# Maxima of the norms ahead of the additions on VectorE, and an output load that is divided and issued sooner, in a four-layer attention and spectral kernel

## The chip, the cores and the metric

The kernel runs on one core of a Trainium2 chip. The metric is the device time of one execution in microseconds (us), as the median of several runs; lower is better. A core has TensorE (matmuls, PE in the profile), VectorE (DVE), ScalarE (ACT) and GpSimd (POOL), which run side by side and wait for each other through semaphores. SyncE (SP) issues most of the transfers between HBM and the on-chip memory (SBUF). Matmul results land in eight banks of PSUM.

## What is computed

x has 2048 rows of 1024 numbers. Four residual layers follow each other: attention, spectral, attention, spectral.

```python
def _A_ref(x, wqkv, wo):
    qkv = (x @ wqkv).reshape(B, S, 3, H, Dh).transpose(2, 0, 3, 1, 4)   # H = 32 heads of 32
    q, k, v = qkv[0], qkv[1], qkv[2]
    scores = jnp.einsum("bhqd,bhkd->bhqk", q, k) * (Dh ** -0.5)
    p = _softmax(scores, axis=-1)
    o = jnp.einsum("bhqk,bhkd->bhqd", p, v)
    return o.transpose(0, 2, 1, 3).reshape(B, S, D) @ wo

def _B_ref(x, w_r, w_i):
    X = jnp.fft.rfft2(x, axes=(-2, -1)) * (w_r + 1j * w_i)
    return jnp.fft.irfft2(X, s=(S, D), axes=(-2, -1))

x = x + _A_ref(_layernorm(x), A_wqkv, A_wo)
x = x + _B_ref(_layernorm(x), B_w_r, B_w_i)      # and both once more
```

The change lies in the attention layers.

## The kernel before

**Groups, chunks, units.** The 32 heads are treated in 8 head groups of 4 (g = 0 to 7). A group's 2048 queries are cut into 4 chunks c of 512, its 2048 keys into 16 tiles kt of 128. One pair (c, kt) is a *unit*, numbered u = 16 c + kt, 64 in a group. `S` computes the scores of a unit for four heads on TensorE (line 720) and their exponentials on ScalarE, in two halves of 128x1024 (line 724). These halves p lie in a pool of 8 buffers, that is four units deep. In every even unit `PV` multiplies the p of the two units before with V (line 730).

**Additions.** The softmax's denominators need the sum of p over the keys. `add` builds it on VectorE, two instructions of 128x1024 a unit (line 741 for the first two tiles of a chunk together, line 743 after that), each into the same accumulator `acc`. The code writes the addition of a unit two units after it: in even units that of the first of the last pair, in odd units that of the second. In the first unit of a chunk both open additions are written.

**Projections beside the attention.** Q, K and V of the next groups are computed in the same loop. `filler` yields these matmuls in pieces and `slots` hands out one piece (a slot) in every odd unit: beside an even group K and Q of the next one and K of the one after, beside an odd group Q of the next and V of the next two. One projection of 512 columns is a *sum* (24 matmuls, line 411 for Q and K, 468 for V), usually spread over three slots. All sums share one PSUM buffer x. For Q and K it is emptied by `split`: the high half on ScalarE (line 215), the low half on VectorE (line 216). For V ScalarE alone empties it (line 472). The next sum's first matmul waits for that.

**Norms.** The exponentials use a bound instead of a running maximum. When the four sums of a group's K or Q are done, `norms` sums the squares over each head with four small matmuls (line 443) into a PSUM buffer of the scores' pool, which has three, and takes their maximum on VectorE (line 445); for Q GpSimd then makes the bias. `ripe` says when: one slot later in even groups, two slots later in odd ones and in group 6. So in groups 1 to 5 they fall in units 25 and 45 (even groups) and 3 and 27 (odd groups), in group 6 in units 43 and 47. `slots` calls them before its piece of matmuls, and that is after the unit's addition is written.

**Order.** Within the main loop the order of TensorE and ScalarE is that of the code. VectorE, GpSimd and SyncE are ordered by the planner, which goes through the program in a model of time and takes for each of them the first instruction in the program that is ready. `tc.issue_after(i)` adds edges to that: what is written inside and runs on the engine of i is put behind i in that engine's order. It is no wait.

**Outputs.** A chunk's output is normalized and stored to HBM (`od`) as a task: `tasks` holds pairs of a least kt and a function, in the order in which they come, and `aside` takes the first of them in an odd unit if its kt is reached and no sum ended in that unit. A chunk is stored some 25 units after its end. In group 6 the loop has 22 slots for the sums of group 7 (8 sums), and then begins with the output projection: `wo_parts` reads outputs of the groups 0 to 6 back with `load_o(c)` (line 523, two transfers of seven groups, one for the high and one for the low halves) and multiplies them by Wo (line 531), 7 matmuls a slot. They are laid over the chunk 2 (or 3) of the normalized input, `xhl`, which the projections read until then. `load_wo` converts Wo into the chunks 0 and 1 of it in the same units.

Of the kernel before, what the change touches and what calls it, by code (L numbers as in the profile page):

```python
# [13 lines left out]
AX = mybir.AxisListType  # L14
# [93 lines left out]
NG, NCH, NKT, NST = 8, 4, 16, 6  # L108
# [110 lines left out]
def run(g):  # L219
    for _ in g:  # L220
        pass
# [106 lines left out]
def attention(nc, tc, layer, ap, xin, yd, wts, wo, cst, dram, flags):  # L328
# [5 lines left out]
    od = dram.tile([2, NG, 128, 2048], F16, name=f"od{layer}")  # L334
# [17 lines left out]
    V, K, Q, bias, nrm, mx = {}, {}, {}, {}, {}, {}  # L352
# [15 lines left out]
    def turn_x(xn):  # L368
        p = psS.tile([128, 2, 512], F32, name="s").rearrange("p h (d n) -> p (h d) n", n=128)
        for d in range(8):  # L370
            nc.tensor.transpose(p[:, d], xn[:, 128 * d:128 * d + 128], cst["ident"])
        return p
# [57 lines left out]
    def ripe():  # L430
        if not left_norms:
            return False
        old = left_norms[0] not in fresh or (g % 2 == 0 and g < NG - 2)
        fresh.clear()
        return old

    def norms():
        kind, g = ph = left_norms.pop(0)
        if g not in mx:
            mx[g] = sm.tile([128, 2], F32, name="mqk")  # L440
        ps = psS.tile([128, 2, 512], F32, name="s")
        for c in range(4):
            nc.tensor.matmul(ps[32 * c:32 * c + 32, 0], cst["bones"], nrm[ph][:, c], start=True, stop=True)
        i = 0 if kind == "k" else 1
        nc.vector.reduce_max(mx[g][:, i:i + 1], ps[:, 0], axis=AX.X)  # L445
        if kind == "q":
            mkbias(g)

    def mkbias(g):
        r = sm.tile([128, 2], F32, name="mall")  # L450
        nc.gpsimd.partition_all_reduce(r, mx[g], 128, bass.bass_isa.ReduceOp.max)
        b = sm.tile([128, 1], F32, name="bpr")
        nc.gpsimd.tensor_tensor(b, r[:, 0:1], r[:, 1:2], op=ALU.mult)
        nc.gpsimd.tensor_tensor(b, b, cst["half"], op=ALU.pow)
        bias[g] = sm.tile([128, 1], F32, name="bias")
        nc.gpsimd.tensor_scalar(bias[g], b, -SCALE / (SQ * SQ), None, op0=ALU.mult)
# [23 lines left out]
    def sums(ph):  # L480
        return 8 if ph[0] == "v" else 4
# [35 lines left out]

    osb, olast = {}, {}

    def load_o(c):  # L520
        osb[c] = xhl[:, 2 + c % 2]
        for i in range(2):
            nc.sync.dma_start(osb[c][:, i, 0:7], od[i, 0:7, :, c * 512:(c + 1) * 512].rearrange("g p n -> p g n"))

    def wo_mm(p, c, t, n, ds, start=True, stop=True, w=512):

# [18 lines left out]
    def wo_part(c, t, dst, nd):  # L545

        x = xres(c, t)
        st = sm.tile([128, 2, 6], F32, name="st")
        for n in range(2):
            p = bank()  # L550
            m = wo_mm(p, c, t, n, range(nd))
            for _ in range(3 * nd - 1):
                next(m)
                yield
            run(m)
            sl = slice(n * 512, n * 512 + 512)
            nc.vector.scalar_tensor_tensor(dst[:, sl], p, 1.0 / (SO * SW), x[:, sl], op0=ALU.mult, op1=ALU.add)
            if nd == 8:
                nc.vector.bn_stats(st[:, n], dst[:, sl])
                if n:  # L560
                    r0 = c * 512 + t * 128
                    nc.sync.dma_start(yd[r0:r0 + 128, :], dst)
                    nc.vector.bn_aggr(mvs[:, 8 * c + 2 * t:8 * c + 2 * t + 2], st)
            yield
# [14 lines left out]
    wo_dst = [ap.x[:, 10 + t if t in SPILL else t] for t in range(8)] + [None] * 2 + [ap.x[:, t] for t in (10, 11)]  # L579

    def wo_parts():
        load_o(0)
        for t in (2, 3, 0, 1, 4, 5, 6, 7, 8, 9, 10, 11):
            if t == 8:
                two = wvp.tile([128, 2, 1024], F32, name="wv")
                wo_dst[8], wo_dst[9] = two[:, 0], two[:, 1]
            yield from wo_part(t // 4, t % 4, wo_dst[t], 8 if t == 11 else 7)
            if t in (0, 5, 9):
                load_o({0: 1, 5: 2, 9: 3}[t])
# [46 lines left out]
    with tc.manual_schedule(engines={mybir.EngineType.PE, mybir.EngineType.DVE, mybir.EngineType.Activation}):  # L636
# [14 lines left out]
        p = turn_x(xn)  # L651
# [13 lines left out]
        p = turn_x(xn)  # L665
# [4 lines left out]
        p = turn_x(xn)  # L670
# [5 lines left out]
        p = turn_x(xn)  # L676
# [60 lines left out]
    def add(g, c, kt):  # L737
        for hf in range(2):
            p, a = P[g, c, kt, hf], acc[c % 2][:, hf]
            if kt == 1:  # L740
                last_add = nc.vector.scalar_tensor_tensor(a, P[g, c, 0, hf], 1e-34, p, op0=ALU.add, op1=ALU.add)  # L741
            elif kt:
                last_add = nc.vector.tensor_add(a, a, p)  # L743
        return last_add if kt else None
# [43 lines left out]
    def times(g, c, r):  # L788
        nc.vector.scalar_tensor_tensor(r, O[g, c], SO, r, op0=ALU.mult, op1=ALU.mult)
        O[g, c] = r  # L790
# [18 lines left out]
    tasks = []  # L809
# [6 lines left out]
    def slots(f, sums, n, steps):  # L816

        while sums:
            k = max(1, int(n / sums + 0.5))
            m = -(-steps // k)  # L820
            for i in range(0, steps, m):
                while ripe():
                    norms()
                for _ in range(min(m, steps - i)):
                    next(f, None)
                n -= 1
                yield sums - (i + m >= steps)
            sums -= 1

    with tc.manual_schedule(engines={mybir.EngineType.PE, mybir.EngineType.Activation}):  # L830
        for g in range(NG):
            todo = sum(sums(ph) for ph in beside.get(g, []))
            sl = slots(fill, todo, 22 if g == NG - 2 else 32, 24)
            wsl = slots(wof, 4, 10, 21)
            for u in range(NCH * NKT):
                c, kt = divmod(u, NKT)
                S(g, c, kt)
                if g == u == 0:
                    run(last_v)
                if kt % 2 == 0:  # L840
                    for w in pend:
                        PV(*w)
                    late = pend
                    pend = []
                    if kt == 0 and late:
                        for w in late:
                            last_add = add(*w)
                        turned, going = going, []
                        if late[1][0] == NG - 1:
                            done = [late[1][:2]]  # L850
                            fin(*done[0])
                        else:
                            going = [*late[1][:2], partials(*late[1][:2])]
                        if turned:
                            with tc.issue_after(last_add.ins):
                                turned[2] = invert_partials(*turned)
                            tasks += [(5, lambda t=turned: times(*t)), (6, lambda t=turned: out(*t[:2]))]
                        if u and g < NG - 2:
                            tasks.append((1, wts.look))
                        late = []  # L860
                for w in late[:1]:
                    last_add = add(*w)
                late = late[1:]
                if kt == 5 and done:
                    out(*done.pop())
                pend.append((g, c, kt))
                if kt % 2 == 0:
                    continue
                quiet, before = kt > 12, todo
                if todo:  # L870
                    todo = next(sl)
                elif g == NG - 2:
                    if left:
                        run(lwo)
                        left = 0
                    if next(wsl, None) is not None and u == NCH * NKT - 1:
                        run(wsl)
                elif g == NG - 1:
                    if u % 4 == 1:
                        with tc.issue_after(last_add.ins):  # L880
                            wts.look()
                    if moments:
                        f, t = moments.pop(0)
                        f(t)
                    if u // 2 in rests:
                        wo_rest(rests[u // 2])
                    for _ in range(share[u // 2]):
                        next(wof)
                if g == NG - 2 and todo <= 6 and left > (8 if todo > 4 else 0):
                    next(lwo)  # L890
                    left -= 1
                if quiet or todo == before:
                    aside(kt)
        for w in pend:
            PV(*w)
        for w in late + pend:
            add(*w)
        run(wof)
    assert not wts.unseen and not wts.cols and not moments
    with tc.manual_schedule(engines={mybir.EngineType.PE}):  # L900
        ps, xs, folds = [], [xres(3, t) for t in range(4)], fold_rests()
# [577 lines left out]
```

## Time and profile before

| | |
|---|---|
| runs (3) | 3708.29, 3709.03, 3711.51 us; median 3709.03 |
| the profiled execution | 3706.65 us, span of its instructions 3704.9 us |
| granted clock of TensorE | 0.997 |
| matmul busy | 3638.7 us (98%) |
| VectorE, ScalarE, GpSimd busy | 3131.2, 2935.2, 637.5 us |
| exponentials (line 724) | 2048, mean 1112 ns, 2171.0 us |
| additions (line 743) | 1792, mean 1218 ns, 2088.4 us |
| first unit of groups 1, 2, 3 in layer 0 | 279.8, 456.3, 630.9 us |

"Busy" is the time in which an engine executes. A line of the time order gives start, duration, engine, line of the kernel, operation, output<-input and the shape, how many like instructions in a row are merged (x2), and in brackets how long the engine stood idle before it and who released it. Instructions of an engine overlap by a little at their ends, so that the distance of two starts is the better price of one. A waits view has, for each waiting line and its releaser, the total us, the number of times and the longest.

### The profile page before, as it was taken

How to read it: one execution, taken by the hardware profiler on the slowest of the kernel's cores; microseconds unless marked ns; L12 is line 12 of the kernel's file. 1: busy time of each engine (PE TensorE's matmuls, PEld its weight loads, DVE VectorE, ACT ScalarE, POOL GpSimd, SP SyncE). 2: the span in 40 equal slices, each digit the busy share in tenths (PEclk: the TensorE clock that was granted, in tenths of full speed). 3: DMA queues.
4: the chain of work that ended last, by engine and by line, in shares of the span. 5: the costliest groups of instructions: out<-in, count | busy, mean ns of one | idle time of the engine just before them, and what ended most of it. 6: DMA issues, size and time to landing. Idle time of an engine off the chain costs nothing.

```text
span 3704.9 us, 80669 instructions
## 1 busy us (share of the span) xinstructions
PE 3638.7 (98%) x32919; PEld 1628.0 (44%) x32919; DVE 3131.2 (85%) x3800; ACT 2935.2 (79%) x3653; POOL 637.5 (17%) x798
## 2 busy tenths in 40 slices
PE   8999999999999999999999999999999999999998
PEld 5333433343343233378953334333433432333888
DVE  7799899989998988886767998999899889788754
ACT  5788888888888867768747888888888888676686
POOL 1021112111111110014420111111111111100243
PEclk9999999999999999999999999999999999999999
DMA  7122232322222442233151232323222334421423
GB/s 197 21 53 54 50 54 53 62 42 56 47 61 50 97 115 70 77 144 106 58 165 21 53 59 51 57 48 59 45 53 52 61 58 95 103 78 69 177 82 108
DMA packets 203551, 274.33 MB, mean 74 GB/s; under 512 B 75809, under 2 KB 122529, under 8 KB 202145
## 3 DMA queue, kind: packets, MB, share of 16 engines
q1 hardware_dynamic: 164208, 195.06, 16.6%
q0 software_dynamic: 37632, 73.43, 14.0%
q8 instruction: 260, 4.26, 0.5%
q14 instruction: 123, 1.00, 0.1%
q10 hardware_dynamic: 1328, 0.59, 0.1%
HBM read 149.00 MB, written 118.42 MB: 72 GB/s over the span
## 4 chain that ended last, share of the span: by engine, by line


## 5 line engine op out<-in xcount | busy, mean ns | idle before, releaser
L724 ACT ACTIVATE p<-s,bias 128x1024 f32<-128x1024 f32 x2048 | 2171.0, 1112 | 467.0 <-PE s L720 449.4
L743 DVE TENSOR_TENSOR R<-R,p 128x1024 f32<-128x1024 f32 x896 | 1044.2, 1218 | 76.2 <-ACT p L724 74.1
L743 DVE TENSOR_TENSOR acc<-acc,p 128x1024 f32<-128x1024 f32 x896 | 1044.2, 1217 | 57.8 <-ACT p L724 55.9
L730 PE MATMUL o<-p,R 128*32 128x512 f32 x8192 | 985.7, 599 | 0.0
L411 PE MATMUL x<-big,wqk 128*128 128x512 f16 x2880 | 676.4, 380 | 2.9 <-ACT R L472 1.6
L720 PEld LDWEIGHTS <-R 32*128 32x128 f16 x12288 | 229.4, 92 | 744.3 <-issue 628.7
L411 PEld LDWEIGHTS <-wqk 128*128 128x128 f16 x3072 | 275.9, 98 | 418.3 <-issue 127.7
L730 PEld LDWEIGHTS o<-p,R 128*32 128x32 f32 x8192 | 213.8, 109 | 524.6 <-issue 524.6
L720 PE MATMUL s<-Q,R 32*128 32x512 f16 x6144 | 425.4, 378 | 5.5 <-DVE mqk L445 5.5
L720 PE MATMUL s<-R 32*128 32x512 f16 x6144 | 426.8, 378 | 0.2
L468 PE MATMUL x<-wv,big 128*128 128x256 f16 x2784 | 330.7, 275 | 4.1 <-DVE R L216 2.2
L468 PEld LDWEIGHTS <-big 128*128 128x128 f16 x3072 | 290.9, 98 | 96.0 <-issue 55.2
L531 PE MATMUL x<-big 128*128 128x512 f16 x1008 | 232.4, 380 | 5.0 <-DMA big<-od 5.0
L749 POOL DMA_DIRECT2D zd<-R x112 | 93.4, 834 | 699.1 <-DVE z L759 289.4
L531 PEld LDWEIGHTS <-big 128*128 128x128 f16 x1428 | 134.2, 98 | 170.1 <-issue 28.4
L749 POOL DMA_DIRECT2D zd<-acc x112 | 92.4, 825 | 645.6 <-DVE z L759 302.5
L741 DVE SCALAR_TENSOR_TENSOR R<-p 128x1024 f32<-128x1024 f32 x64 | 75.5, 1221 | 97.5 <-ACT p L724 97.5
L752 POOL DMA_DIRECT2D zd<-zd x112 | 89.4, 798 | 367.0 <-DMA zd<-zd 154.3
L1143 DVE TENSOR_TENSOR H<-G,H 128x512 f16<-128x512 f32 (+1 forms) x68 | 46.8, 689 | 99.9 <-ACT H L1142 99.7
L741 DVE SCALAR_TENSOR_TENSOR acc<-p 128x1024 f32<-128x1024 f32 x64 | 75.8, 1221 | 45.6 <-ACT p L724 45.6
L1085 ACT COPY U<-ps 64x256 f32<-64x256 f32 (+1 forms) x272 | 97.2, 357 | 8.1 <-PE ps L1092 3.0
L1085 ACT COPY B<-ps 64x256 f32<-64x256 f32 (+1 forms) x272 | 97.1, 357 | 5.6 <-PE ps L1092 2.1
(459 smaller groups left out, 3291.5 us busy)
## 6 DMA issues: line engine op xcount, KB each, us to landing
zd<-R POOLq DMA_DIRECT2D x112, 256.0 KB, 4.1
zd<-acc POOLq DMA_DIRECT2D x112, 256.0 KB, 4.2
wst<-in_wp SPq DMA_DIRECT2D x96, 256.0 KB, 3.4
R<-y SPq DMA_DIRECT2D x32, 512.0 KB, 5.8
w<-in_w SPq DMA_DIRECT2D x60, 256.0 KB, 2.7
zt<-zr SPq DMA_DIRECT2D x224, 64.0 KB, 2.7
od<-ohl SPq DMA_DIRECT2D x56, 256.0 KB, 2.4
big<-od SPq DMA_DIRECT2D x16, 896.0 KB, 6.4
```

The source lines that it names most:

```text
L411: nc.tensor.matmul(ps, a, b, start=i == 0, stop=i == 23)
L468: nc.tensor.matmul(ps[:, j], x[c][:, d, o:o + 128], w[:, n, d], start=i == 0, stop=i == 23)
L531: nc.tensor.matmul(p, a, b, start=start and d == ds[0] and i == 0, stop=stop and d == ds[-1] and i == 2)
L720: nc.tensor.matmul(s[h // 2][:, h % 2], K[g][r, a, kt * 128:kt * 128 + 128], Q[g][r, b, c * 512:c * 512 + 512], start=i == 0, stop=i == 2)
L724: nc.scalar.activation(p, s[hf], AF.Exp, bias=bias[g], scale=SCALE / (SQ * SQ))
L730: nc.tensor.matmul(O[g, c][32 * h:32 * h + 32], V[g][:, kt, 32 * h:32 * h + 32], P[g, c, kt, h // 2][:, h % 2], start=kt == 0, stop=kt == ...
L741: last_add = nc.vector.scalar_tensor_tensor(a, P[g, c, 0, hf], 1e-34, p, op0=ALU.add, op1=ALU.add)
L743: last_add = nc.vector.tensor_add(a, a, p)
L749: nc.gpsimd.dma_start(z, a[32 * j:32 * j + 32].rearrange("p a j n -> p (a j n)"), max_dma_last_dim=2048, **({"accum_op": ALU.add} if j els ...
L752: nc.gpsimd.dma_start(z[0:n], z[n:2 * n], accum_op=ALU.add, max_dma_last_dim=2048)
L1085: nc.scalar.copy(ov[64 * r:64 * r + 64, a0:a0 + m, x], tl[64 * x:64 * x + 64, :m, r])
L1143: nc.vector.tensor_sub(lo, gs, hi)
```

## The change

`norms` returns the instruction of the maximum. It is no longer called by `slots` but by the main loop in each odd unit, ahead of that unit's addition, and the addition is written behind an edge to the maximum. The matmuls of the norm keep their place on TensorE: after the scores, before the slot's piece.

`load_o` takes a range of groups. The load for chunk 0 is no longer the first step of `wo_parts`: the outputs of the groups 0 to 5 are asked for in group 6 when two of the eight sums are left (the last sum that reads that part of `xhl` has ended then, in unit 33; the first slot of the output projection is unit 45), and those of group 6 as a task with a least kt of 8. The loads of the other chunks stay as they are.

```diff
@@ norms
-        nc.vector.reduce_max(mx[g][:, i:i + 1], ps[:, 0], axis=AX.X)
+        top = nc.vector.reduce_max(mx[g][:, i:i + 1], ps[:, 0], axis=AX.X)
         if kind == "q":
             mkbias(g)
+        return top
@@ load_o
-    def load_o(c):
+    def load_o(c, gs=slice(0, NG - 1)):
         osb[c] = xhl[:, 2 + c % 2]
         for i in range(2):
-            nc.sync.dma_start(osb[c][:, i, 0:7], od[i, 0:7, :, c * 512:(c + 1) * 512].rearrange("g p n -> p g n"))
+            nc.sync.dma_start(osb[c][:, i, gs], od[i, gs, :, c * 512:(c + 1) * 512].rearrange("g p n -> p g n"))
@@ wo_parts
-        load_o(0)
@@ slots
-                while ripe():
-                    norms()
@@ the main loop
+                top = None
+                while kt % 2 and ripe():
+                    top = norms()
                 for w in late[:1]:
-                    last_add = add(*w)
+                    with tc.issue_after(top.ins) if top else nullcontext():
+                        last_add = add(*w)
                 late = late[1:]
@@ the main loop, after the slot
+                if g == NG - 2 and todo <= 2 < before:
+                    load_o(0, slice(0, NG - 2))
+                    tasks.append((8, lambda: load_o(0, slice(NG - 2, NG - 1))))
                 if g == NG - 2 and todo <= 6 and left > (8 if todo > 4 else 0):
                     next(lwo)
```

## Prediction

> **What bounds the kernel now.** I read the page first, then TensorE's waits, then the time order of VectorE and TensorE around a norm and around the first load of outputs.
>
> ```profile
> PE 3638.7 (98%) x32919; PEld 1628.0 (44%) x32919; DVE 3131.2 (85%) x3800; ACT 2935.2 (79%) x3653; POOL 637.5 (17%) x798
> ```
> ```profile
> PE s L720 <- DVE mqk L445: 5.5, 6, 1.5
> PE x L531 <- DMA big<-od: 5.0, 2, 3.2
> ```
>
> TensorE is busy for 98% of the span, so what delays it delays the end. The change goes at two of its waits: scores (L720) that wait for the maximum L445, 5.5 us in 6 places, and output-projection matmuls (L531) that wait for outputs read back, 5.0 us in 2 places. VectorE's 85% looks like room, but it is a mean. What decides is how much room there is next to a norm.
>
> There are 28 norms in the main loops (14 a layer), in four kinds of place that repeat. I quote one of each. First, unit 3 of an odd head group (6 norms: groups 1, 3 and 5 of two layers), VectorE and then TensorE:
>
> ```profile
> 284.43 2.36 DVE L741 SCALAR_TENSOR_TENSOR R<-p 128x1024 f32<-128x1024 f32 x2 [1.76 <-ACT p L724]
> 287.02 2.36 DVE L743 TENSOR_TENSOR R<-R,p 128x1024 f32<-128x1024 f32 x2 [0.23 <-ACT p L724]
> 289.30 0.68 DVE L445 TENSOR_REDUCE mqk<-s 128x1 f32<-128x512 f32 x1
> 289.90 2.35 DVE L743 TENSOR_TENSOR R<-R,p 128x1024 f32<-128x1024 f32 x2
> 292.56 2.36 DVE L743 TENSOR_TENSOR R<-R,p 128x1024 f32<-128x1024 f32 x2 [0.31 <-ACT p L724]
> 295.23 2.36 DVE L743 TENSOR_TENSOR R<-R,p 128x1024 f32<-128x1024 f32 x2 [0.31 <-ACT p L724]
> ...
> 313.27 0.68 DVE L216 SCALAR_TENSOR_TENSOR R<-x,R 128x512 f16<-128x512 f32 x1
> ```
> ```profile
> 288.38 0.40 PE L443 MATMUL s<-sq,bones 128*32 128x512 bf16 x4
> ...
> 314.74 1.47 PE L411 MATMUL x<-big,wqk 128*128 128x512 f16 x6
> ```
>
> VectorE adds each unit's two halves as soon as ScalarE has made them: the waits in brackets are for the exponentials p of L724, made just before. The code writes the addition of a unit two units later, but VectorE's order is the planner's, and the planner lets it run ahead. The addition that unit 3 writes is that of unit 1 (L741), and it began at 284.43, 4.4 us before the norm's matmuls ended at 288.78. Unit 2's followed at 287.02. The last row, L216, is the low half of a projection. TensorE's next projection (314.74) needs the only buffer x, which this L216 (ended 313.95) frees. It came 0.8 us early.
>
> **The edge on the additions, place by place.** The edge puts the maximum ahead of the addition that its unit writes. Each sum adds into the last, so every later addition stands behind the maximum too. What is queued behind the waiting maximum is then two units' additions that VectorE did earlier while it had nothing else.
>
> *Unit 3, odd groups.* The maximum can start at about 288.85 and takes 0.60 (289.30 to 289.90). The four held halves take 1.14 each (289.30 - 287.02 over two), 4.56 in all. The next addition starts at 294.0 instead of 289.90: VectorE is 4.1 us later. The two idle spots of 0.31 take up 0.6 before 313.27. If L216 keeps its place, it is 3.5 late, 0.8 of it covered: TensorE stands 2.7 us.
>
> Whether L216 keeps its place is the planner's choice. Second place, unit 25 of an even group (6 norms), VectorE, then TensorE, then ScalarE:
>
> ```profile
> 518.16 2.36 DVE L743 TENSOR_TENSOR acc<-acc,p 128x1024 f32<-128x1024 f32 x2 [0.25 <-ACT p L724]
> ...
> 521.37 2.35 DVE L743 TENSOR_TENSOR acc<-acc,p 128x1024 f32<-128x1024 f32 x2
> 523.64 0.68 DVE L445 TENSOR_REDUCE mqk<-s 128x1 f32<-128x512 f32 x1
> 524.24 2.35 DVE L743 TENSOR_TENSOR acc<-acc,p 128x1024 f32<-128x1024 f32 x2
> ...
> 528.24 9.16 DVE L743 TENSOR_TENSOR acc<-acc,p 128x1024 f32<-128x1024 f32 x8
> 537.32 0.68 DVE L216 SCALAR_TENSOR_TENSOR Q<-x,Q 128x512 f16<-128x512 f32 x1
> ```
> ```profile
> 522.11 0.40 PE L443 MATMUL s<-sq,bones 128*32 128x512 bf16 x4
> ...
> 538.15 2.76 PE L411 MATMUL x<-big,wqk 128*128 128x512 f16 x12
> ```
> ```profile
> 535.06 0.60 ACT L215 ACTIVATE Q<-x 128x512 f16<-128x512 f32 x1
> ```
>
> ScalarE's half was done at 535.66, yet L216 started at 537.32, 1.66 us later, longer than an addition (1.14): at least one addition that began after L216 was ready stands ahead of it. So the plan reckons VectorE as faster than it is, and has fewer of the additions open than the chip has. After the change the plan catches up its own delay sooner than the chip does, and puts L216 nearly where it was. I take it half an addition (0.57) earlier on average. Unit 3 costs 2.1 us, six times: **12.8**. The bounds are 0 (L216 put ahead of the whole backlog) and 2.7.
>
> *Unit 25, even groups.* The norm ends at 522.51. Both units' additions, begun at 518.16 and 521.37, are held. The maximum runs from 522.6 to 523.2, the held halves to 527.75, against 524.24 before: 3.5 us later. From there to 537.32 no row has a wait, and L216 (ended 538.00) was only 0.15 early: at most 3.35, with half an addition off 2.8, three times in layer 0: **8.4**. In layer 1 the same L216 is earlier:
>
> ```profile
> 2034.48 0.68 DVE L216 SCALAR_TENSOR_TENSOR Q<-x,Q 128x512 f16<-128x512 f32 x1
> ```
> ```profile
> 2036.16 2.12 PE L411 MATMUL x<-big,wqk 128*128 128x512 f16 x9
> ```
>
> It has 1.0 us of cover (2035.16 to 2036.16), which leaves at most 2.5, with half an addition off 1.9, three times: **5.7**.
>
> *Unit 45, even groups* (6 norms), VectorE and TensorE:
>
> ```profile
> 580.43 7.11 DVE L743 TENSOR_TENSOR R<-R,p 128x1024 f32<-128x1024 f32 x6
> ...
> 590.39 2.36 DVE L741 SCALAR_TENSOR_TENSOR acc<-p 128x1024 f32<-128x1024 f32 x2 [2.07 <-ACT p L724]
> 592.66 0.68 DVE L216 SCALAR_TENSOR_TENSOR R<-x,R 128x512 f16<-128x512 f32 x1
> ```
> ```profile
> 578.03 0.40 PE L443 MATMUL s<-sq,bones 128*32 128x512 bf16 x4
> ...
> 594.34 1.90 PE L411 MATMUL x<-big,wqk 128*128 128x512 f16 x8
> ```
>
> The same working (578.43 + 0.1 + 0.6 + 4.56 = 583.7, against 580.43) gives 3.3 us. The idle 2.07 takes most of it, and L216 had 1.0 of cover: 0.2 us, or 2.3 if the idle does not help. I take 0.7, near the low end, six times: **4.2**.
>
> *Unit 27, odd groups* (6 norms). Here the maximum did stop TensorE, in layer 0 and layer 1:
>
> ```profile
> 353.38 0.39 PE L720 MATMUL s<-Q,R 32*128 32x512 f16 x2
> ...
> 355.25 0.82 PE L720 MATMUL s<-Q,R 32*128 32x512 f16 x10 [1.48 <-DVE mqk L445]
> ```
> ```profile
> 2202.83 0.82 PE L720 MATMUL s<-Q,R 32*128 32x512 f16 x10 [0.36 <-DVE mqk L445]
> ```
>
> The twelve matmuls of L720 take 0.82 in one piece; here they ran from 353.38 to 356.07, 1.87 late, which is the wait of 1.48 and 0.39 of restart. In layer 1 it is 0.36 and the same 0.39. With the maximum ahead of the additions all of it goes: 3 x 1.87 + 3 x 0.75 = **7.9 gained**. VectorE's delay costs nothing here, because the sums that follow are those of V, which ScalarE alone evicts (L472). The 4 norms of group 6 I put at 0.5 us together, between 0 and 1. ScalarE itself does not come to wait: no row of its waits has L724 waiting for VectorE, and the eight buffers of p are four units deep, over 10 us at the 2.65 a unit of the first rows (289.90, 292.56, 295.23), against 4.1 of delay. Outside the loops (norms at the start of a layer) nothing moves.
>
> **The load of outputs.** Layer 0, then the clock in that window, then layer 1:
>
> ```profile
> 1285.43 1.40 PE L531 MATMUL x<-big 128*128 128x512 f16 x5 [3.20 <-DMA big<-od]
> 1286.76 1.46 PE L720 MATMUL s<-R 32*128 32x512 f16 x12
> 1288.15 2.73 PE L730 MATMUL o<-p,R 128*32 128x512 f32 x16
> ```
> ```profile
> 1285.40:1289.00 3.60, 3.57 (x21) 0.90 (x25) 0.00 (x0) 0.74 (x1) 0.00 (x0) 0.64 0.00 0
> ```
> ```profile
> 3128.61 1.25 PE L531 MATMUL x<-big 128*128 128x512 f16 x5 [1.77 <-DMA big<-od]
> 3129.80 0.82 PE L720 MATMUL s<-R 32*128 32x512 f16 x12
> 3130.55 1.92 PE L730 MATMUL o<-p,R 128*32 128x512 f32 x16
> ```
>
> The wait was for the second of two DMAs. After the change six of seven head groups' outputs are asked for when two sums are left, unit 33 instead of 45. That is 12 units of 2.65, some 30 us, ahead, and both waits go: 3.20 and 1.77. Layer 0's wait also lowered the granted clock to 0.64: the next rows are 0.15, 0.64 and 0.81 longer than layer 1's, 1.6 us that go too. **6.6 gained**. The chunk that the load overwrites is free exactly then, so on SP's queue (the weight loads of Wo, the divisors and the outputs stand there) it waits at most for the last matmul of that unit. The seventh group's piece comes as a task in unit 45, is wanted by the 19th projection matmul, two slots later, and costs nothing. If it came late, TensorE would stand for as long as now.
>
> [...] The trace shows the drop at 3.20 and none at 1.77, and I go by it.
>
> **Sum.** Costs 12.8 + 8.4 + 5.7 + 4.2 + 0.5 = 31.6; gains 7.9 + 6.6 = 14.5; net 17.1 us slower. The profiled execution took 3706.65, so 3723.8. The runs' median 3709.03 lies 2.4 higher and gives 3726.1.
>
> **Rivals.** *Faster:* the planner puts each L216 ahead of the held additions (it is ready, and stands earlier in the program than the newest of them). The backlog then lies on VectorE alone, which catches up in the idle places, and only the gains are left: 3709.03 - 14.5 = 3694.5. It decides from the point at which the plan's backlog at an L216 is three additions or more. For it: the plan sees the hold as well. Against it: the 1.66 us at 535.66. Chance 0.13. [...] *No change to be told:* L216 stands about an addition and a half earlier than before; the costs halve to about 15 and meet the gains: 3709 to 3710. Chance 0.13. *Worse:* every L216 keeps its place, 6 x 2.7 + 3 x 3.35 + 3 x 2.5 + 6 x 2.3 + 1 = 48.5, less 14.5: 34 slower, 3743. Waits of over 3 us would also lower the clock, as above, 1.6 each in three places. Chance 0.06. *That it doesn't do what it says:* in all the places quoted the maximum stands behind additions that the edge would hold, so it must bite; I give that nothing of its own.
>
> **How the numbers follow.** Forecast 0.68 (8 to 27 us slower), the rivals 0.13, 0.13 and 0.06. A measurement of this kernel can tell about 0.2%, 7.4 us. Faster by more: 0.13. Within: 0.13. Slower by more: 0.74. The range takes in the forecast, most of the equal case and part of the worse one: 3705 to 3738, leaving out the faster rival and the top.
>
> **What would show it.** Right: L445 within 0.2 us of its matmuls' end in every norm, two units' additions right behind it, and VectorE idle for 1 to 6 us ahead of it; no TensorE wait on mqk or on od; new TensorE waits of L411 for L216 in units 7 to 13 of odd groups and in unit 31 (perhaps 51) of even ones. Wrong: no such waits and a shorter main loop; or ScalarE's L724 waiting for additions.

## The result and the profile after

The changed kernel takes 3738.4 us, the median of 6 runs (3737.48 to 3742.48), beside 3709.32 for the kernel before. The ratio is 1.008, with a 95% interval of 1.0067 to 1.0093: 29 us slower. The profiled execution took 3737.48 us, its span is 3735.7.

The first part of the page, and then the waits of TensorE (who waits, for whom, total us, times, longest us):

```profile
PE 3643.0 (98%) x32919; PEld 1629.9 (44%) x32919; DVE 3128.5 (84%) x3800; ACT 2934.7 (79%) x3653; POOL 666.1 (18%) x798
```
```profile
PE x L411 <- DVE R L216: 21.4, 14, 2.4
PE x L411 <- DVE Q L216: 15.3, 6, 3.5
```

The busy times of TensorE, VectorE and ScalarE are the same to within 5 us (GpSimd's is 28.6 higher), and the page alone would not tell where the time went. The waits do. Both rows of before are gone: none for the maximum, none for the outputs. In their place TensorE waits 36.7 us for L216, the low half of a projection; before, that row had 1.3 us in 2 places, which are still among the 20.

VectorE's own waits say where this begins. Before, then after:

```profile
DVE mqk L445 <- PE s L443: 8.0, 5, 2.7
```
```profile
DVE mqk L445 <- PE s L443: 91.6, 32, 6.7
```

VectorE now stands idle 91.6 us in front of the maxima, as the order forces it to wait for each norm's matmuls while additions are ready behind. Unit 3 of group 1 after, VectorE, TensorE, and ScalarE:

```profile
291.61 0.69 DVE L445 TENSOR_REDUCE mqk<-s 128x1 f32<-128x512 f32 x1 [6.26 <-PE s L443]
292.22 2.35 DVE L741 SCALAR_TENSOR_TENSOR R<-p 128x1024 f32<-128x1024 f32 x2
294.49 9.17 DVE L743 TENSOR_TENSOR R<-R,p 128x1024 f32<-128x1024 f32 x8
303.57 0.68 DVE L216 SCALAR_TENSOR_TENSOR R<-x,R 128x512 f16<-128x512 f32 x1
```
```profile
291.06 0.40 PE L443 MATMUL s<-sq,bones 128*32 128x512 bf16 x4
...
304.31 1.89 PE L411 MATMUL x<-big,wqk 128*128 128x512 f16 x8 [2.43 <-DVE R L216]
```
```profile
298.71 0.60 ACT L215 ACTIVATE R<-x 128x512 f16<-128x512 f32 x1
```

The maximum waits 6.26 us and comes 0.15 us after its matmuls. Then the additions of units 1 to 5 run without a gap. L216 was ready at 299.31, when ScalarE's half ended, and starts 4.3 us later, in the same place behind unit 5's additions that it had before. TensorE stands 2.43 us.

Unit 25 to 31 of group 2 after, VectorE, TensorE, ScalarE, and the granted clock (the number after the five engines) in the 3 us behind the wait:

```profile
526.13 0.69 DVE L445 TENSOR_REDUCE mqk<-s 128x1 f32<-128x512 f32 x1 [2.01 <-PE s L443]
...
535.28 9.16 DVE L743 TENSOR_TENSOR acc<-acc,p 128x1024 f32<-128x1024 f32 x8
544.36 0.68 DVE L216 SCALAR_TENSOR_TENSOR Q<-x,Q 128x512 f16<-128x512 f32 x1
```
```profile
545.09 4.44 PE L411 MATMUL x<-big,wqk 128*128 128x512 f16 x12 [3.52 <-DVE Q L216]
```
```profile
538.46 0.60 ACT L215 ACTIVATE Q<-x 128x512 f16<-128x512 f32 x1
```
```profile
545.00:548.00 3.00, 2.91 (x8) 1.10 (x8) 3.00 (x5) 0.00 (x0) 0.00 (x0) 0.57 0.00 0
```

Again eight halves of additions stand right ahead of L216, as before. The wait is 3.52 us, and after it the clock is 0.57: the twelve matmuls that took 2.76 us before take 4.44.

The load after, at the first projection matmuls of layer 0:

```profile
1298.56 0.83 PE L720 MATMUL s<-R 32*128 32x512 f16 x12
1299.31 1.69 PE L532 MATMUL x<-big 128*128 128x512 f16 x7
```

All seven run in one piece. The whole of that gain came.

### The profile page after: what moved, and what is told of

Its sections match the earlier page's. It is cut to its first block, busy times and chain, and to the rows that moved or that the text cites. A ratio compares the mean times of both kernels' runs of the same rounds, so it can differ in the third digit from the quotient of the medians.

```text
span 3735.7 us, 80609 instructions
## 1 busy us (share of the span) xinstructions
PE 3643.0 (98%) x32919; PEld 1629.9 (44%) x32919; DVE 3128.5 (84%) x3800; ACT 2934.7 (79%) x3653; POOL 666.1 (18%) x798
## 4 chain that ended last, share of the span: by engine, by line
## 5 line engine op out<-in xcount | busy, mean ns | idle before, releaser
L724 ACT ACTIVATE p<-s,bias 128x1024 f32<-128x1024 f32 x2048 | 2171.0, 1112 | 496.1 <-PE s L720 465.1
L411 PE MATMUL x<-big,wqk 128*128 128x512 f16 x2880 | 682.8, 383 | 38.4 <-DVE R L216 21.4
L741 DVE SCALAR_TENSOR_TENSOR R<-p 128x1024 f32<-128x1024 f32 x64 | 75.5, 1221 | 68.0 <-ACT p L724 67.9
L1097 PE MATMUL ps<-cbi,H 128*128 128x256 f16 (+1 forms) x792 | 99.1, 273 | 3.6 <-DVE H L1148 2.8
```

What stands on the lines that cost most here:

```text
L411: nc.tensor.matmul(ps, a, b, start=i == 0, stop=i == 23)
L724: nc.scalar.activation(p, s[hf], AF.Exp, bias=bias[g], scale=SCALE / (SQ * SQ))
L1097: nc.tensor.matmul(out, l, r, start=k == 0, stop=k == len(mm_) - 1)
```

## Experiments

The theory after the result: the edge alone costs, by holding two units' additions while VectorE idles, so that low halves come late; the load gains. The rivals: the load is part of the loss; the earlier place of the call in the program is; VectorE is so full that any hold comes back.

**The load alone.** The kernel before with the new `load_o` and its two new calls in place of the old one, and nothing else.

> The divided, earlier load alone; norms as before. Theory (the edge on the additions costs, the load gains): 3702.4 us, that is 6.9 under before: no TensorE wait on od, units 45 and 46 of group 6 shorter by 3.5 and 1.4 us in layer 0 and by 1.9 in layer 1, everything else as before. Rival (the load, issued amid other transfers, delays something and is part of the loss): no faster than before, 3709 or more.

3702.66 us, ratio 0.9984 (0.9975 to 0.9993). TensorE has no wait on od. By the starts of the units' scores, units 45 and 46 of group 6 are 3.52 and 1.44 us shorter in layer 0, unit 45 is 1.95 in layer 1, and no other unit of the main loops moved by 0.1, but for unit 1 of layer 0 (0.8 longer). The load is no part of the loss.

**The maxima alone.** The changed kernel with the old load:

```diff
     def wo_parts():
+        load_o(0)
...
-                if g == NG - 2 and todo <= 2 < before:
-                    load_o(0, slice(0, NG - 2))
-                    tasks.append((8, lambda: load_o(0, slice(NG - 2, NG - 1))))
```

> The maxima with their edge alone; the load as before. Theory: the loss of the changed kernel and the gain of the load on top, 3738.4 + 6.9 = 3745.3 us, with the same TensorE waits for the low halves (about 36 us in all). Rival (the load is part of the loss): under 3738.

3738.96 us, ratio 1.0082 (1.0067 to 1.0097): as slow as the changed kernel, where 7 us more were expected. The waits for L216 are the same, 21.4 and 15.3 us. The miss is the load's, whose wait shrank by itself:

```profile
PE x L532 <- DMA big<-od: 2.6, 2, 2.1
```

It had been 5.0. In layer 0 the store of the output that the load needs was issued at 1290.09, 2.4 us before the norm's matmuls of unit 43 ended; in the kernel before it was 1.1 us (1274.51 against 1275.62). VectorE has additions held behind the maximum and makes the output's low half that much sooner. With the clock loss behind it the old load still costs 4.6 us by the starts of the units (the main loops grew by 33.6 us over before, those of the changed kernel by 29.0). The two medians differ by 0.6, which their intervals cannot tell from 4.6. So the medians of this pair do not measure the load's worth on top of the edge.

**No edge.** The changed kernel with norms called ahead of the addition's line, but:

```diff
                 for w in late[:1]:
-                    with tc.issue_after(top.ins) if top else nullcontext():
-                        last_add = add(*w)
+                    last_add = add(*w)
```

> The changed kernel without the edge: norms are still called by the main loop ahead of the addition's line, but no addition is put behind the maximum. Theory (only the edge reorders VectorE, since the planner takes what is ready): additions run ahead as before, the six waits for the maximum come back, 3702.4 us like the load alone. Rival (the earlier place of the call in the program reorders VectorE or the scores' PSUM buffers): near the changed kernel, 3730 or more.

3702.47 us, ratio 0.9983 (0.9974 to 0.9992), the load alone to 0.2 us, and the waits for the maximum are back in full:

```profile
PE s L720 <- DVE mqk L445: 5.5, 6, 1.5
```

Calling norms earlier in the program does nothing, good or bad. All of the loss is the edge's.

**The edge in unit 27 alone.**

```diff
-                    with tc.issue_after(top.ins) if top else nullcontext():
+                    with tc.issue_after(top.ins) if top and g % 2 and u == 27 else nullcontext():
```

> The changed kernel with the edge only in unit 27 of odd groups, the one place where TensorE had waited for the maximum and where the sums that follow are V's. Theory: the gains alone, 3709.3 - 7.8 - 6.9 = 3694.6 us, no TensorE wait on the maximum and none that is new. Rival (VectorE has no room anywhere, so a hold always comes back later, here at the first sums of the next group): 3702 us or more, with new waits for low halves in units 1 to 13 of groups 2, 4 and 6.

3693.45 us, ratio 0.9958 (0.9944 to 0.9971): 15 us faster than before, and the best kernel of this study. Unit 28 of each odd group is 1.87 us shorter in layer 0 and 0.74 in layer 1, 7.8 together; no new wait of the main loops is in the list. VectorE and TensorE at unit 27 of group 1:

```profile
351.99 0.69 DVE L445 TENSOR_REDUCE mqk<-s 128x1 f32<-128x512 f32 x1 [2.25 <-PE s L443]
...
355.99 13.71 DVE L743 TENSOR_TENSOR acc<-acc,p 128x1024 f32<-128x1024 f32 x12
```
```profile
353.69 0.83 PE L720 MATMUL s<-Q,R 32*128 32x512 f16 x12
```

VectorE idles 2.25 us for the norm and then works off its additions without a pause, the last twelve halves, six units' worth, in one row. TensorE does not wait for it meanwhile, as the sums beside them are V's. Here the hold is free; the rival, that a hold always comes back, falls for this place.

**The edge one unit later.** The addition of the next unit gets the edge, so one more unit's addition goes ahead of the maximum (a first `top = None` ahead of the loops is left out here):

```diff
-                top = None
-                while kt % 2 and ripe():
-                    top = norms()
                 for w in late[:1]:
-                    with tc.issue_after(top.ins) if top else nullcontext():
+                    with tc.issue_after(top.ins) if top and kt % 2 == 0 else nullcontext():
                         last_add = add(*w)
+                top = None
+                while kt % 2 and ripe():
+                    top = norms()
```

> As the changed kernel, but the edge is put on the addition that the next unit writes, so that VectorE keeps one more unit's addition ahead of the maximum and stands idle for less. Theory (what costs is that two units' additions are held while VectorE idles): the hold shrinks from about 4 us to under 2, most of the new waits go, and the six waits for the maximum go or shrink as well: about 3700 us. Rival (any edge between maxima and additions costs, VectorE being full): nearer to the changed kernel, 3720 or more.

3699.47 us, ratio 0.9973 (0.9963 to 0.9982): 3 under the load alone, 6 over the edge in unit 27 alone. Unit 3 of group 1:

```profile
285.01 2.36 DVE L741 SCALAR_TENSOR_TENSOR R<-p 128x1024 f32<-128x1024 f32 x2 [1.76 <-ACT p L724]
289.51 0.69 DVE L445 TENSOR_REDUCE mqk<-s 128x1 f32<-128x512 f32 x1 [2.14 <-PE s L443]
```

Unit 1's additions (L741) go ahead of the maximum again. The idle time before it falls from 6.26 to 2.14 us, unit 7's wait in this group from 2.43 to 0.16, unit 31's in group 2 from 3.52 to 1.25, and unit 51's is gone. The six waits for the maximum in unit 28 are gone too; one of 0.44 is new in unit 48 of group 6. It is the depth of the hold that costs, not the maximum's place.

**The edge in unit 3 alone**, with `g % 2 and u == 3` as the condition.

> The edge only in unit 3 of odd groups (6 norms). Theory: the low half of the next sum keeps its place behind the held additions, TensorE waits 2.4 us in each of the six unit 7s, so 3702.5 + 6 x 2.6 = 3718 us if no wait lowers the clock, up to 1.6 more for each that does, 3728 at most. The clock loss should differ from place to place with the same 2.4 us wait. Rival (the clock loss belongs to the place, layer 1): just the three of layer 1, 3723.

3721.51 us, ratio 1.0035 (1.0021 to 1.0048), 19 over the load alone. Each of the six units 7 has its wait of 2.43. The granted clock in the 3 us behind each of them, groups 1, 3, 5 of layer 0, then of layer 1:

```profile
302.00:305.00 3.00, 2.98 (x24) 1.06 (x27) 3.00 (x4) 0.30 (x1) 0.78 (x1) 1.00 0.20 27
655.70:658.70 3.00, 3.00 (x8) 1.01 (x7) 3.00 (x4) 0.00 (x0) 0.78 (x1) 0.53 0.19 29
1011.50:1014.50 3.00, 2.99 (x24) 1.05 (x27) 3.00 (x4) 0.31 (x1) 0.78 (x1) 1.00 0.16 22
2156.95:2159.95 3.00, 3.00 (x12) 0.97 (x15) 3.00 (x4) 0.00 (x0) 0.42 (x2) 0.63 0.16 22
2510.60:2513.60 3.00, 3.00 (x24) 1.05 (x27) 3.00 (x4) 0.32 (x1) 0.35 (x1) 1.00 0.20 27
2862.80:2865.80 3.00, 3.00 (x24) 1.06 (x27) 3.00 (x4) 0.32 (x1) 0.76 (x1) 1.00 0.15 22
```

The clock fell behind two of six equal waits, in group 3 of layer 0 and group 1 of layer 1, where the changed kernel's profile has it behind all three of layer 1 and none of layer 0. The loss does not belong to the place.

**The low half first.** The changed kernel, and behind each norm (not in unit 27) the next low half of a Q or K sum is noted, and the first addition written after it is put behind it:

```diff
-        split(nc, t[:, 0], t[:, 1], ps, SQ / (SX * SW))
+        _, low = split(nc, t[:, 0], t[:, 1], ps, SQ / (SX * SW))
+        if armed:
+            armed.clear()
+            holds.append(low)
...
                     top = norms()
+                    if u != 27:
+                        armed.append(u)
                 for w in late[:1]:
+                    hold = holds.pop() if holds and w[2] else None
                     with tc.issue_after(top.ins) if top else nullcontext():
-                        last_add = add(*w)
+                        with tc.issue_after(hold.ins) if hold else nullcontext():
+                            last_add = add(*w)
```

> The changed kernel, and the first addition written after the first low half that follows a norm (not in unit 27) is put behind that low half. Theory (the place of the low half behind held additions is what TensorE waits for): the waits in units 31 and 51 of even groups shrink, those in unit 7 do not get longer by more than half a us, 3715 to 3725 us. Rival (the low half is late because VectorE is full, its place does not matter): 3738 or more.

3722.02 us, ratio 1.0034 (1.0023 to 1.0045). In even groups the waits of units 31 and 51 are gone, with 0.6 to 0.7 us left in units 41 and 61 of layer 0: there the place of the low half is what TensorE waits for. In odd groups the wait of unit 7 went as well, and came back larger at the next sum, unit 13, whose low half no edge puts ahead:

```profile
PE x L411 <- DVE R L216: 20.5, 11, 2.9
```
```profile
296.27 0.69 DVE L216 SCALAR_TENSOR_TENSOR R<-x,R 128x512 f16<-128x512 f32 x1 [0.23 <-ACT R L215]
...
302.35 9.17 DVE L746 TENSOR_TENSOR R<-R,p 128x1024 f32<-128x1024 f32 x8
311.43 0.68 DVE L799 TENSOR_TENSOR ohl<-zt,ohl 128x512 f16<-128x512 f32 x1
312.04 4.62 DVE L746 TENSOR_TENSOR R<-R,p 128x1024 f32<-128x1024 f32 x4
316.58 0.68 DVE L216 SCALAR_TENSOR_TENSOR R<-x,R 128x512 f16<-128x512 f32 x1
```

L216 runs at 296.27, as soon as ScalarE is done. But the backlog is only put off: from there to the next L216 no row has a wait, and TensorE stands 2.9 us in unit 13, six times, with a lower clock behind each (over the whole profiled execution the granted clock is 0.994, and 0.997 before). So the time lies in the range that was expected in part by luck: the waits that were to stay in unit 7 went, and longer ones came. Odd groups have no room for the hold here; in even groups most of it is absorbed.

**The edge in unit 25 alone**, with `g % 2 == 0 and u == 25`.

> The edge only in unit 25 of even groups (6 norms). Theory: waits in unit 31 as in the changed kernel, 2 x 1.7 + 2 x 3.5 + 2 x 2.4 = 15.2 us, and a lower clock after the two of 3.5 us (1.7 each) and perhaps after others: 3702.5 + 15.2 + 3.5 = 3721 us, 3718 to 3725. Rival (the waits need the holds of the other places too, as VectorE's backlog carries over): under 3712.

3725.47 us, ratio 1.004 (1.0025 to 1.0055), 23 over the load alone. The waits of unit 31 are those of the changed kernel to 0.01 us (2 x 1.72, 2 x 3.52, 2 x 2.39, in all 15.3), so the places add up and need no backlog from each other. The clock fell behind all four longer ones (0.994 over the whole execution), which makes this 4 us more than expected.

## Why the prediction was wrong in size and right in kind

The direction and the chain held: the edge holds two units' additions, VectorE idles, L216 comes late, TensorE waits for x. The time lies 0.4 us above the range, and the loss is 29 where 17 was forecast. By terms, in us; measured is what the units around each place grew by, from the starts of their scores in the two traces:

| term | forecast | TensorE's waits | with the clock and all, measured |
|---|---|---|---|
| unit 3, odd groups | 12.8 | 14.6 | 20.2 |
| unit 25, even groups | 14.1 | 15.3 | 19.0 |
| unit 45, even groups | 4.2 | 5.5 | 4.8 |
| unit 27, odd groups | -7.9 | | -7.8 |
| group 6's norms | 0.5 | 0.5 | 0.6 |
| the load | -6.6 | | -6.9 |
| sum | 17.1 | | 29.9 |

(The main loops as a whole grew by 29.0; 0.6 of the difference is that the units 26 of even groups became 0.1 us shorter each, the rest is in pieces under 0.5 us. Unit 45 was not run alone: its row is read from the two traces.)

- The step that failed is the clock. The prediction took the drop behind a 3.20 us wait as a gain, and put the same drop behind the new waits only into the rival *worse*, "1.6 each in three places". Five waits of the changed kernel's profile lowered the clock, by 1.64 to 1.74 us each, 8.5 in all, and three of these were only 2.43 long. That is two thirds of the missing 12.
- The other third lies in the waits themselves: 35.4 us where 31.1 was forecast for the three places, 3.0 of it in units 3 and 25. Here "I take it half an addition (0.57) earlier on average" failed. No L216 that TensorE waited for came earlier: the same eight halves stand ahead of it in unit 31, and in unit 7 the same unit 5. The reason given was right (the plan reckons VectorE as faster than it is, 1.66 us at 535.66), the discount had no row behind it.
- The discount took 6.8 us off the units 3 and 25. The forecast there fell short by only 3.0, since the waits from which the discount was taken were 3.8 too high. The largest piece, 1.6, is unit 31 of group 0 in layer 0, for which group 2's row stood, with 3.35. Group 0 has a norm in unit 25 too, but before the change VectorE idles twice there (0.24 and 0.25 us) and L216 has 1.0 us of cover, so its wait is 1.72 where those of groups 2 and 4 are 3.52. That two errors partly cancel here is luck.
- The rival *worse* had the mechanism, every L216 in its place and the clock drop on top, at a chance of 0.06. It came out too high (34 without the clock, where 29 was measured with it), as it put unit 45 at 2.3 each (0.9 measured) and had group 2's wait in all of layer 0.
- In odd groups the wait was put at unit 13; it came at unit 7, the first sum behind the norm, with the same size: 4.1 less 0.6 of idle and 0.9 of cover.
- Unit 45 was chosen near the low end; layer 0 has 1.49 and layer 1 0.35, mean 0.9, and unit 46 of layer 0 gave 0.36 back. Unit 27 and the load were right to 0.3 us. (The load goes out only 8 units sooner, at 1270.13 in unit 35 where it was 1276.88 in unit 43, and not 12; that was enough.) The low half's place decides as the *faster* rival had it, as the seventh experiment shows in even groups. The planner did not choose that place.
- *No change to be told* and *faster* fall: in VectorE's order in the changed kernel none of the L216 of units 7, 31 and 51, for which TensorE waits, came earlier.
- The prediction read that L724 never waits for VectorE. The waits have one such row, 0.6 us in 3 places, but it is the same before and after, so that nothing hung on it.

## What to carry to other kernels

In this kernel an order edge that put a short, late instruction ahead of ready work cost VectorE the idle time in front of it (91.6 us, where it was 8.0), and TensorE paid for that where it next needed VectorE and had no cover. Look for that next consumer, not at the engine's mean load. Put the edge only where the wait it removes is seen and where what follows does not need the engine: here unit 27 gave all of the edge's gain, and units 3, 25 and 45 nearly all of its loss. And price a new wait on TensorE with the clock that it may cost (1.64 to 1.74 us each behind five of the waits here), if a profile shows such a loss; the next section says when it came here.

## What the runs showed of the hardware

All TensorE waits of over 1 us in the main loops of the ten profiles, and whether the units behind them ran longer at a lowered clock (by 1.64 to 1.74 us in the changed kernel's): of 30 waits of 1.2 to 1.8 us none; one of 2.05 did; of 24 of 2.4 us 10 did; of 13 of 2.9 to 3.5 us all did. Equal waits of 2.43 us at the same place fell on both sides in different kernels, as the six rows of the sixth experiment show.

The traces also show where the two kinds differ. In the records of before and after the granted clock is 1.0 or 0.5. But for the last of each, in which the span ends, the records at 0.5 are 3.413 us long (three before, seven after) or 6.827 (one in each), and within a trace they start multiples of 3.4133 us apart, to 0.03 us. From trace to trace the places differ: one starts at 1286.41 us before and one at 545.43 after, which are no multiple of it apart. Here are two waits of 2.43 us of the sixth experiment (group 3 of layer 0, then group 5 of layer 1), each with two stretches of that length, cut at 655.86, where the clock fell, and at multiples of 3.4133 us from there; they hold the end of the wait and what follows (length, busy time of TensorE, and after the five engines the clock):

```profile
652.44:655.86 3.41, 0.98 (x17) 0.41 (x14) 3.41 (x5) 2.49 (x3) 0.82 (x1) 1.00 0.28 38
655.86:659.27 3.41, 3.41 (x12) 1.05 (x14) 3.41 (x5) 0.00 (x0) 0.78 (x1) 0.50 0.16 24
2860.87:2864.28 3.41, 1.48 (x7) 0.68 (x7) 3.41 (x6) 1.66 (x2) 0.78 (x1) 1.00 0.24 37
2864.28:2867.69 3.41, 3.41 (x42) 0.86 (x40) 3.41 (x4) 2.12 (x2) 0.97 (x1) 1.00 0.12 17
```

The first wait falls whole into one stretch: TensorE idles for 2.43 us of it, and the next stretch runs at 0.50. The second wait is cut in two: the stretch has 1.93 us of idle time, and the next one runs at 1.00. The traces of before and after, cut in this way from 35 us after their start on, agree: 12 stretches at full clock had 1.99 us or more of idle TensorE, and each was followed by one at half clock; the other 2123 had at most 1.77, and none was. Half of 3.413 us is 1.7, an estimate of what such a stretch at 0.5 loses; behind a wait 1.64 to 1.74 were measured. That all 13 waits of 2.9 us and more lowered the clock is in part luck, by an estimate from these counts: cut in its middle, a wait of 2.9 us would leave 1.45 in each of two stretches, less than the 1.77 behind which the clock stayed.
